# w2's gradient computed transposed, in two sets of PSUM banks, and turned in the last stage; bulk loads spread; turned queries stored sooner

## The chip, the cores and the metric

The kernel runs on one core of a Trainium2 chip. The metric is the device time of the whole program in microseconds (us); before the change three runs gave 822.75 to 823.58 us, median 823.29. A core has a matrix engine (TensorE, PE in the profile; its weight loads are PEld), three engines for other arithmetic (VectorE = DVE, ScalarE = ACT, GpSimd = POOL) and SyncE (SP), which here only issues transfers. Each engine works through its own list of instructions in order. PE writes to PSUM, eight banks of 512 floats on each of 128 partitions; ACT or DVE must copy a finished sum out before its bank can be used again. Transfers between DRAM and the on-chip memory SBUF are issued by SP, ACT or POOL and run beside the engines; some of them transpose what they move.

## The reference, cut to what matters

One transformer block (linear attention with 32 heads, then a gated MLP) is computed forward, and then its gradients for the input and five weight matrices. Sequence 2048, model width D = 640, MLP width F = 1728, all bf16.

```python
x = A_x
h = x + _A_ref(_layernorm(x, axis=-1), A_wqkv, A_wo)
h2 = h + _B_ref(_layernorm(h, axis=-1), B_w1, B_w3, B_w2)

def _B_ref(x, w1, w3, w2):
    gate = jnp.einsum("bsd,df->bsf", x, w1)
    up = jnp.einsum("bsd,df->bsf", x, w3)
    h = _silu(gate) * up
    out = jnp.einsum("bsf,fd->bsd", h, w2)
    return out
```

The change concerns above all the gradient of w2, an array of 1728 x 640: `h` transposed (1728 x 2048) times the gradient of the output (2048 x 640), a sum over the 2048 positions.

## The kernel before

The order of the work is written out by hand (`tc.manual_schedule()`): what stands later in the code comes later in the list of its engine. Tiles come from pools; a tile that takes over the place of another waits until all users of the old one are done. Positions are cut into 16 tiles of 128 (`t`), D into 5 chunks of 128 (`DT`), F into 13 chunks of 128 and one of 64.

The stages, with their times in the profiled execution:

1. **Projections** (0 to about 73 us, L458 to L638). For each position tile: statistics on DVE (`stat`, L480), normalising (`p1_norm`, L246; tiles 10, 12 and 14 on ACT, the others on DVE), turning (tiles 0 to 7 on PE, tiles 8 to 15 by a transposing transfer, L250), the projection on PE (`p1_mm`, L273), exp and relu on ACT (`phi`, L289). The list of DVE's steps beside tile t is `v_steps` (L508): S is `stat`, N `p1_norm`, R a remaining piece of `phi`; A, B and L place a normalising step before the query tile, after it, or last. SP's loads of x (L194, L461, L464), wqkv, w1, w3 (`w13`, L499), w2 and wo stand in front of this loop, in its dictionary `trickle` (L505) and after it (L591 to L594). `kvT_block` (L443) needs the last third of wqkv (`load_wq(4, 6)`) and the turned sums `mT`.
2. **Attention, second part** (73 to 98 us, the list given to `run`, L945). `q_late` projects the last query tiles into `pkx`; `q_out` (L724) stores tiles 10 to 13 from there through POOL's queue; `f2_wT` makes the matrix `Wp`, which `f2_half` multiplies with the turned queries. Then the pool `p1`, which holds `pkx`, is released, and the pool `pa` of the MLP takes its place.
3. **MLP forward and the gradients inside it** (98 to 340 us, L1003).
4. **Gradient of w2** (340.54 to 399.44 us, L1041 to L1111). `load_hh` turns four column blocks of the stored `h` into tiles `hb` (position on the partitions). For each of 13 chunks of 128 columns of F two sums of 16 matmuls are made: a block of `hb` as weights, 320 columns of the output gradient `g2` as the moving side. ACT copies each [128 x 640] result and stores it to the output `out_6`. The last 64 columns are done in `gw2_tail`, two halves side by side in the array. SP loads the next stage's weights (`load_w13`) and gradients (`load_gg`) meanwhile.
5. **Backward through the MLP and the attention** (399.44 to 699.5 us, L1257 to L1545). `b_ghn` (L1134) begins it, with PSUM tiles in the banks of stage 4. Its first steps need `ggb[0]` and the turned w1 and w3; `b_ln` then needs the loads of `b_load` (L1129).
6. **Gradients of w1 and w3** (699.5 to 816 us, L1548 to L1562). Seven blocks of up to 496 columns; for each block five jobs of 16 matmuls (`grad_job`), copied out by ACT and stored through ACT's queue. After each block SP loads the block after the next, by a transposing transfer, into the tile that has just come free.

Every transfer of SP and ACT counts up, when it lands, one of eight counters, which the program uses in turn; a transfer may not start before the one that used its counter last has landed. POOL's transfers have eight of their own.

Of the kernel before, what the change touches and what calls it, by code (L numbers as in the profile page):

```python
# [9 lines left out]
P = 128  # L10
BF16 = mybir.dt.bfloat16
F32 = mybir.dt.float32
# [6 lines left out]
S, D, H, F = 2048, 640, 32, 1728  # L19
DH = D // H  # L20
ST, DT = S // P, D // P
FT, FP = 14, 1792
FL = F - 13 * P
W, SC, TPC = 512, 4, 4
HD = D // 2
NG = 27
# [29 lines left out]
def kernel(  # L56
# [19 lines left out]
    V, A, T, G, SY = nc.vector, nc.scalar, nc.tensor, nc.gpsimd, nc.sync  # L76
# [20 lines left out]
    kvT_d = dram.tile([D, D], BF16, name="kvT_d")  # L97
    dwoT_d = dram.tile([D, D], BF16, name="dwoT_d")
    hn_d = dram.tile([S, D], BF16, name="hn_d")
    hh_d = dram.tile([F, S], BF16, name="hh_d")  # L100
# [81 lines left out]
    def load_wq(a, b):  # L182
        dma(out=wqkv[:, :, a * HD:b * HD], in_=wq_v[:, :, a * HD:b * HD])

    def load_x(a, b):
        dma(out=x_sb[:, a:b, :], in_=xS[:, a:b, :])
# [6 lines left out]
    load_x(3, 4)  # L193
    load_x(4, 8)  # L194

# [31 lines left out]
    def load_w13(c0, c1):  # L227
        def go1():
            dma(out=w1[:, c0:c1, 0:F], in_=rows(B_w1)[:, c0:c1, :])

        def go3():
            dma(out=w3[:, c0:c1, :], in_=rows(B_w3)[:, c0:c1, 0:F - FL])
        return [go1, go3]
# [198 lines left out]
    def m_end(m, js=(0, 1)):  # L432
        mb = mbs[:, m % 4, :]
        acc = macc[m]
        for j in js:
            A.copy(out=mb[:, j * HD:(j + 1) * HD], in_=acc[j][:, 0:HD])
        if m < 2:
            A.copy(out=Z[:, m:m + 1], in_=acc[1][:, HD:HD + 1])
            z_diag(m)
        if m < DT - 1:  # L440
            dmaT(out=mT[:, :, m * P:(m + 1) * P], in_=mb)
# [18 lines left out]
    load_g2T(0)  # L460
    load_x(8, 12)  # L461
    load_w2T(2 * P, 4 * P)
    load_wq(0, 2)
    load_x(12, ST)  # L464
    def warm_up(n, warm):
# [36 lines left out]
    def load_wo():  # L502
        dma(out=wo[:], in_=A_wo.rearrange("(c p) n -> p c n", p=P))

    trickle = {4: w13[0], 5: w13[1], 9: lambda: load_wq(4, 6), 12: w13[2], 14: w13[3]}  # L505

    R = None
    v_steps = {1: (R, ("N", 4)), 2: (("S", 5), R, ("N", 5)), 3: (("S", 6), R, ("N", 6), ("C", 0)),  # L508
               4: (("S", 7), R, ("N", 7), ("S", 8)), 5: (R, ("N", 8), ("S", 9)), 6: (R, ("N", 9), ("S", 10)),
               7: (("S", 11), R, R, ("A", 10), ("L", 11)), 8: (("S", 12), R, R, ("S", 13)),  # L510
               9: (("N", 13), R, ("S", 14), ("B", 12)), 10: (R, R, ("S", 15)), 11: (R, ("B", 14), ("L", 15))}
    V_OPS = {"S": stat, "N": p1_norm, "C": p1_scale}
# [8 lines left out]

    outs = {7: ((xn_out, 0, dma),), 8: ((group_out, 0),), 12: ((group_out, 1), (xn_out, 1, dma)), 13: ((group_out, 2),)}

# [66 lines left out]
    m_end(1)  # L590
    load_wo()  # L591
    group_out(SC - 1)
    for go in w13[4:]:
        go()  # L594
    z_late((2, 3, 4), big())
# [5 lines left out]
    m_part(2, range(10, ST))  # L601
    m_end(2)
    dmaG(out=m_v[:, 0, :], in_=mbs[:, 0, :])
    r_head(0)
# [336 lines left out]
    def kv3():  # L941
# [5 lines left out]
        (f2_wT, 4), (phi_rest,), (q_late, 14), (r_T, 4), (r_head, 5), (r_prod, 7),  # L947
        (mlp_ghh, 4),
        (q_late, 15), (w2_room,), (sig_table,), (f2_half, 0, 0), (f2_half, 1, 0), (f2_half, 2, 0), (f2_half, 3, 0), (mlp_ghh, 5),
        (f2_half, 0, 1), (r_store, 4, 5), (f2_half, 1, 1), (f2_hn, 0), (r_store, 5, 6), (f2_half, 2, 1), (f2_hn, 1),  # L950
        (f2_half, 3, 1), (f2_m_out,), (q_out, 10, 14),
        (f2_half, 4, 0, True), (mlp_ghh, 6), (f2_half, 4, 1, True), (f2_half, 5, 0, True), (r_red, 6, (0,)), (f2_hn, 2), (f2_hn, 3),
# [28 lines left out]
    def r_end(t):  # L981
        r_scale(t)
        r_out(t)

    r_steps = [{0: ((load_x, 6, 8),), 1: ((r4_out, 0, 2),), 2: ((r_load, 8),), 3: ((load_w2T, 10 * P, F),), 4: ((r_load, 9), (r4_out, 2, 4)),
                5: ((r_store, 7, 8),),
# [53 lines left out]

    hb, blk = {}, [(0, 512), (512, 512), (1024, 512), (1536, 192)]  # L1041

    def load_hh(b):
        f0, fw = blk[b]
        hb[b] = U2.tile([P, ST, 512], BF16, name="hb", tag="ABCA"[b])
        for a, n in ((0, 2 * P), (2 * P, 2 * P)) if b == 0 else ((0, fw),):
            dmaT(out=hb[b][:, :, a:a + n], in_=hh_d[f0 + a:f0 + a + n, :])

# [23 lines left out]
    def load_gg(j, c0, c1, q=dma):  # L1072
        if c0 == 0:
            ggb[j] = ba.tile([P, NG, 2 * P], BF16, name="ggb", bufs=2)
        q(out=ggb[j][:, c0:c1, :],
            in_=gg_d[c0 * P:c1 * P, j * 2 * P:(j + 1) * 2 * P].rearrange("(c p) w -> p c w", p=P))

    def gw2_tail():

        gt = ps.tile([P, 2, 512], F32, name="gt", tag="gw", bufs=4)  # L1080
        for t in range(ST):
            for j in range(2):
                T.matmul(gt[j * FL:(j + 1) * FL, 0, 0:HD], lhsT=hb[3][:, t, P:P + FL],
                         rhs=g2[:, t, j * HD:(j + 1) * HD], start=(t == 0), stop=(t == ST - 1))
        ob = br.tile([P, HD], BF16, name="gts")
        A.copy(out=ob[:], in_=gt[:, 0, 0:HD])
        for j in range(2):
            A.dma_start(out=out_6[F - FL:F, j * HD:(j + 1) * HD], in_=ob[j * FL:(j + 1) * FL, :])

    for fc in range(FT - 1):  # L1090
        b, i = divmod(fc, 4)
        if fc == FT - 2:
            gw2_tail()
        acc = ps.tile([P, 2, 512], F32, name="gw", bufs=4)
        for j in range(2):
            for t in range(ST):
                T.matmul(acc[:, j, 0:HD], lhsT=hb[b][:, t, i * P:(i + 1) * P], rhs=g2[:, t, j * HD:(j + 1) * HD],  # L1097
                         start=(t == 0), stop=(t == ST - 1))
        ob = br.tile([P, D], BF16, name="gw2o", bufs=2)
        A.copy(out=ob[:].rearrange("p (j n) -> p j n", j=2), in_=acc[:, :, 0:HD])  # L1100
        A.dma_start(out=out_6[fc * P:(fc + 1) * P, :], in_=ob[:])
        if fc == 3:
            load_hh(3)
        if fc == 5:
            load_w13()
        if fc == 8:
            load_gg(0, 0, NG)
        if fc == 11:
            load_gg(1, 0, NG)
    ps.release()  # L1110
# [440 lines left out]
    dmaT(out=g_h[:, 0:DT, :], in_=dwoT_d[:, :])  # L1551
    dma(out=out3S, in_=g_h[:, 0:DT, :])
    for i, (f0, f1) in enumerate(blocks):
        n = f1 - f0
        for m in range(DT):
            last = (i, m) == (len(blocks) - 1, DT - 1)
            for a, b in ((0, n - P), (n - P, n)) if last else ((0, n),):
                c = (a + b) // 2
                halves = ((a, c), (c, b)) if i * DT + m < 5 else ((a, b),)
                out = [(x + y - a, z + y - a, to) for y, w in halves for x, z, to in both_grads(m, f0 + y, f0 + w)]  # L1560
                grad_job(hnN, m, lambda t: gb[i][:, t, a:b], b - a, out, A.dma_start)
        load_block(i + 2)  # L1562
    ps.release()
    ex.release()
# [34 lines left out]
```

## Time and profile before

| what | value |
|---|---|
| median of 3 runs | 823.29 us |
| the profiled execution, time | 820.91 us |
| its span, first to last instruction | 819.1 us |
| granted clock of PE | 1.000 |
| PE busy | 814.1 us, 5420 matmuls |
| DVE, ACT, POOL busy | 452.4, 323.6, 130.9 us |
| gradient of w2, 416 matmuls of 320 columns | 56.8 us busy |
| its tail, 32 matmuls | 2.29 us of the chain |
| last stage, 576 matmuls | 116.65 us of the chain |

Times are from the start of the span. The profile has, among others, busy times by engine, a chain of work that is followed back from the last instruction, groups of instructions, timelines of each engine, and for every transfer the time from its issue to its landing. A busy PE is one that has a matmul under way; whether it runs at its pace is seen from the time between the starts of matmuls.

### The profile page before, as it was taken

Reading aid. Unit: us, or ns where it says so; the run is one execution under the profiler, and the core shown is the slowest. Engines: PE = TensorE matmul, PEld = TensorE weight load, DVE = VectorE, ACT = ScalarE, POOL = GpSimd, SP = SyncE. Lnnn points to the kernel's source line nnn. Section 1 sums busy time; section 2 is a strip of 40 time slices with the busy share of each in tenths; the row PEclk is TensorE's granted clock in tenths of the full one; section 3 lists DMA queues with packets and bytes.
Section 4 is the critical chain, followed back from the end, with each engine's and each line's share of the span. In section 5 each row is a group of like instructions: output and inputs, shape, how many; then the busy total and the mean of one; then the engine's idle time right before and its main releaser. Section 6 shows DMA issues by size and latency. Waiting matters only on the chain.

```text
span 819.1 us, 13944 instructions
## 1 busy us (share of the span) xinstructions
PE 814.1 (99%) x5420; PEld 512.8 (63%) x5420; DVE 452.4 (55%) x973; ACT 323.6 (40%) x603; POOL 130.9 (16%) x193
## 2 busy tenths in 40 slices
PE   9999999999999999999999999999999999999998
PEld 6677544555555555777777777777777777544444
DVE  7859987998898566300057777772781544200000
ACT  7856688665565666011122212222212334211111
POOL 2233333333222212100001111110220000000000
PEclk9999999999999999999999999999999999999999
DMA  9899699796485556999977877259974997967751
GB/s 264 219 290 239 166 244 327 225 245 173 127 211 156 169 170 167 222 261 226 257 176 180 211 197 200 58 107 187 287 195 93 181 194 159 239 164 186 160 141 36
DMA packets 323873, 157.88 MB, mean 193 GB/s; under 512 B 242784, under 2 KB 317056, under 8 KB 323808
## 3 DMA queue, kind: packets, MB, share of 16 engines
q1 hardware_dynamic: 281040, 116.18, 61.6%
q0 software_dynamic: 7328, 24.48, 8.7%
q10 hardware_dynamic: 35440, 16.34, 7.7%
q8 instruction: 42, 0.69, 0.4%
q14 instruction: 23, 0.19, 0.1%
HBM read 47.09 MB, written 51.13 MB: 120 GB/s over the span
## 4 chain that ended last, share of the span: by engine, by line
PE 96%; DVE 2%; ACT 1%; issue 0%; DMA 0%; POOL 0%; ACTq 0%; DVEq 0%
PE mm L394 20%; PE job L1346 20%; PE ghn L1142 14%; PE gxn L1515 8%; PE gw L1097 7%; PE o L910 4%; PE o L856 3%; PE gwo L1230 3%; PE big L267 3%; PE gr L1199 3%; PE dkv L1452 3%; PE macc L429 2%; PE at L654 2%; PE mm L267 1%; PE dkv L1380 1%; DVE st L147 1%
## 5 line engine op out<-in xcount | busy, mean ns | idle before, releaser
L1346 PE MATMUL job<-gb,hnN 128*128 128x496 bf16 (+3 forms) x576 | 116.8, 366 | 0.0
L1142 PEld LDWEIGHTS <-ggb 128*128 128x128 bf16 x864 | 84.5, 98 | 32.8
L1346 PEld LDWEIGHTS <-hnN 128*128 128x128 bf16 x576 | 55.8, 98 | 61.0
L394 PE MATMUL mm<-pqT,w 128*128 128x512 bf16 x405 | 93.8, 379 | 0.1
L394 PEld LDWEIGHTS <-w 128*128 128x128 bf16 x540 | 52.5, 98 | 63.4 <-issue 1.4
L1350 ACT CAST obs<-job 128x496 bf16<-128x496 f32 (+4 forms) x56 | 28.5, 510 | 123.7 <-PE job L1346 120.9
L1142 PE MATMUL ghn<-w13a,ggb 128*128 128x320 bf16 x448 | 63.5, 299 | 0.0
L1157 DVE SCALAR_TENSOR_TENSOR wb<-gs,hnb 128x640 f32<-128x640 bf16 x16 | 13.2, 825 | 88.7 <-ACT gs L1154 88.7
L1142 PE MATMUL ghn<-w13b,ggb 128*128 128x320 bf16 x416 | 61.4, 299 | 0.0
L394 PE MATMUL mm<-g2T,w2T 128*128 128x512 bf16 x240 | 59.6, 379 | 0.0
L1097 PE MATMUL gw<-g,hb 128*128 128x320 bf16 x416 | 56.8, 299 | 0.0
L1207 POOL TENSOR_TENSOR sz<-Zb,g_h 128x640 f32<-128x640 bf16 x16 | 20.2, 1261 | 197.7 <-DVE g_h L1208 197.7
L1097 PEld LDWEIGHTS <-hb 128*128 128x128 bf16 x416 | 40.6, 98 | 16.0 <-issue 0.3
L419 ACT CAST ghh<-mm 128x512 bf16<-128x512 f32 x48 | 28.3, 589 | 47.7 <-PE mm L394 40.1
L793 ACT ACTIVATE sig<-mm 128x512 bf16<-128x512 f32 x56 | 33.9, 605 | 26.4 <-PE mm L394 21.1
L1154 ACT ACTIVATE gs<-ghn 128x640 bf16<-128x640 f32 x16 | 11.3, 704 | 78.8 <-PE ghn L1142 73.9
L394 PEld LDWEIGHTS <-w2T 128*128 128x128 bf16 x260 | 25.4, 98 | 23.4
L267 PEld LDWEIGHTS <-pqT 128*128 128x128 bf16 x320 | 30.7, 98 | 13.7 <-ACT pqT L259 1.5
L267 PE MATMUL big<-wqkv,pqT 128*128 128x320 bf16 x250 | 38.6, 299 | 0.6 <-ACT pqT L259 0.3
L1346 PEld LDWEIGHTS <-g 128*128 128x128 bf16 x320 | 31.0, 98 | 11.5
L829 DVE TENSOR_TENSOR gate<-gate,sig 128x1024 bf16<-128x1024 bf16 x28 | 19.3, 689 | 33.2 <-ACT gate L804 30.5
L910 PE MATMUL o<-w,hhT 128*128 128x320 bf16 x224 | 35.0, 299 | 0.0
(219 smaller groups left out, 1369.9 us busy)
## 6 DMA issues: line engine op xcount, KB each, us to landing
hh_d<-hhT SPq DMA_DIRECT2D x24, 256.0 KB, 2.7
gg_d<-gate POOLq DMA_DIRECT2D x24, 256.0 KB, 4.3
gg_d<-ghh POOLq DMA_DIRECT2D x24, 256.0 KB, 3.4
ggb<-gg_d SPq DMA_DIRECT2D x6, 896.0 KB, 5.4
ggb<-gg_d ACTq DMA_DIRECT2D x6, 832.0 KB, 5.7
ggb<-gg_d SPq DMA_DIRECT2D x2, 1728.0 KB, 12.7
x_sb<-in_A_x_dram SPq DMA_DIRECT2D x5, 640.0 KB, 5.9
pk_d<-pk_all SPq DMA_DIRECT2D x4, 640.0 KB, 6.6
```

What stands on the lines that cost most here:

```text
L267: T.matmul(acc, lhsT=pqT[:, c, t * P:(t + 1) * P], rhs=wqkv[:, c, n0:n0 + HD], start=(c == 0), stop=(c == DT - 1))
L394: T.matmul(acc[:], lhsT=w[:, c, fc * P:(fc + 1) * P], rhs=rhs[:, c, :], start=(c == 0), stop=(c == DT - 1))
L419: A.copy(out=ghh[n // 2][:, n % 2, :], in_=acc[:])
L793: A.activation(sig[:, i, :], gp[:], AF.Sigmoid)
L856: T.matmul(accs[i, j][:, 0:HD], lhsT=hhT[c][:, fc, i * P:(i + 1) * P], rhs=w2[:, fc, j * HD:(j + 1) * HD], start=(first and fc == 0), stop ...
L910: T.matmul(o2["ps"][:, 0:HD], lhsT=hhT[c][:, fc, i * P:(i + 1) * P], rhs=w2[:, fc, j * HD:(j + 1) * HD], start=(fc == 0), stop=(fc == FT - 1))
L1097: T.matmul(acc[:, j, 0:HD], lhsT=hb[b][:, t, i * P:(i + 1) * P], rhs=g2[:, t, j * HD:(j + 1) * HD], start=(t == 0), stop=(t == ST - 1))
L1142: T.matmul(acc[:, j, 0:HD], lhsT=ggb[t // 2][:, k, lo:lo + P], rhs=rhs[:, j * HD:(j + 1) * HD], start=(k == 0), stop=(k == NG - 1))
L1199: T.matmul(gr[t][:, j, 0:HD], lhsT=ghT[t][:, c, :], rhs=wT2[:, c, j * HD:(j + 1) * HD], start=(c == 0), stop=(c == DT - 1))
L1346: T.matmul(acc[:, 0:n], lhsT=lhs[:, t, m * P:(m + 1) * P], rhs=rhs(t), start=(t == 0), stop=(t == ST - 1))
L1350: A.copy(out=ob, in_=acc[:, 0:n])
L1515: T.matmul(acc[:, j, 0:HD], lhsT=g, rhs=wqT[:, k, j * HD:(j + 1) * HD], start=(k == 0), stop=(k == 14))
```

## The change

- **Gradient of w2 turned round.** The four column blocks become 256, 448, 512 and 512 wide. For each block and each of the 5 chunks of D one sum of 16 matmuls is made, now with 128 columns of `g2` as weights and the whole block of `hb` as the moving side: 20 sums of up to 512 columns, with no tail of its own. The result is the gradient transposed; ACT copies and stores it to a scratch array `gw2T_d` in DRAM. The sums use two sets of four PSUM banks (`gw0`, `gw1`). POOL clears the padding of the block of 448.
- **Last stage.** After blocks 0 to 3 of the last stage SP loads a part of `gw2T_d` back by a transposing transfer into a free part of `g_h` (`gw2_turn`), and one block later stores it to `out_6` (`gw2_out`). Two more jobs store their result in halves.
- **Loads.** x comes as tiles 4-5, 6-9, 10-15 instead of 4-7, 8-11, 12-15. The second piece of w3 is cut in two. `load_wq(4, 6)` moves from tile 9 of the loop to the place of `load_wo`, `load_wo` and the last weight pieces move to after `m_end(2)`, one weight piece moves from tile 14 to after the loop. The first store of `pk` comes one tile later. Tile 14 is normalised by ACT before the query tile instead of after it. Two steps of the MLP's load list change places.
- **Query store.** `q_out(10, 14)` comes after `r_prod(7)` instead of at the end of the attention's list.

```diff
-    load_x(4, 8)
+    load_x(4, 6)
...
-        def go3():
+        def go3(c0=c0, c1=c1):
...
-    load_x(8, 12)
+    load_x(6, 10)
     load_w2T(2 * P, 4 * P)
     load_wq(0, 2)
-    load_x(12, ST)
+    load_x(10, ST)
...
-    trickle = {4: w13[0], 5: w13[1], 9: lambda: load_wq(4, 6), 12: w13[2], 14: w13[3]}
+    trickle = {4: w13[0], 5: lambda: w13[1](0, 1), 6: lambda: w13[1](1, 2), 12: w13[2]}
...
-               9: (("N", 13), R, ("S", 14), ("B", 12)), 10: (R, R, ("S", 15)), 11: (R, ("B", 14), ("L", 15))}
+               9: (("N", 13), R, ("S", 14), ("B", 12)), 10: (R, R, ("S", 15)), 11: (R, ("A", 14), ("L", 15))}
...
-    outs = {7: ((xn_out, 0, dma),), 8: ((group_out, 0),), 12: ((group_out, 1), (xn_out, 1, dma)), 13: ((group_out, 2),)}
+    outs = {7: ((xn_out, 0, dma),), 9: ((group_out, 0),), 12: ((group_out, 1), (xn_out, 1, dma)), 13: ((group_out, 2),)}
...
-    load_wo()
+    load_wq(4, 6)
     group_out(SC - 1)
-    for go in w13[4:]:
-        go()
+    w13[3]()
...
     m_end(2)
+    load_wo()
+    for go in w13[4:]:
+        go()
...
-        (mlp_ghh, 4),
+        (q_out, 10, 14), (mlp_ghh, 4),
...
-        (f2_half, 3, 1), (f2_m_out,), (q_out, 10, 14),
+        (f2_half, 3, 1), (f2_m_out,),
...
-    hb, blk = {}, [(0, 512), (512, 512), (1024, 512), (1536, 192)]
+    hb, blk = {}, [(0, 256), (256, 448), (704, 512), (1216, 512)]
...
+    for n in range(len(blk) * DT):
+        b, m = divmod(n, DT)
+        f0, fw = blk[b]
+        tag = "gw0" if n // 4 in (0, 2) or n in (16, 17) else "gw1"
+        acc = ps.tile([P, 512], F32, name="gw", tag=tag, bufs=4)
         for t in range(ST):
+            T.matmul(acc[:, 0:fw], lhsT=g2[:, t, m * P:(m + 1) * P], rhs=hb[b][:, t, 0:fw], start=(t == 0),
+                     stop=(t == ST - 1))
+        ob, fp = br.tile([P, 512], BF16, name="gw2o", bufs=3), (fw + P - 1) // P * P
+        if fp > fw:
+            G.memset(ob[:, fw:fp], 0.0)
+        A.copy(out=ob[:, 0:fw], in_=acc[:, 0:fw])
+        A.dma_start(out=gw2T_d[m * P:(m + 1) * P, b * 512:b * 512 + fp], in_=ob[:, 0:fp])
+        if n == 4:
             load_hh(3)
+        if n == 9:
             load_w13()
+        if n in (12, 15):
+            load_gg((n - 12) // 3, 0, NG)
...
+    turned = [DT, DT + 2, DT + 6, 0]
+
+    def gw2_turn(b):
+        n = (blk[b][1] + P - 1) // P
+        dmaT(out=g_h[:, turned[b]:turned[b] + n, :], in_=gw2T_d[:, b * 512:b * 512 + n * P])
+
+    def gw2_out(b):
+        f0, fw = blk[b]
+        n, k = fw // P, turned[b]
+        dma(out=out_6[f0:f0 + n * P, :].rearrange("(k p) d -> p k d", p=P), in_=g_h[:, k:k + n, :])
+        if fw % P:
+            dma(out=out_6[f0 + n * P:f0 + fw, :], in_=g_h[0:fw % P, k + n, :])
...
-                halves = ((a, c), (c, b)) if i * DT + m < 5 else ((a, b),)
+                halves = ((a, c), (c, b)) if i * DT + m < 7 else ((a, b),)
...
         load_block(i + 2)
+        if 0 < i <= 4:
+            gw2_out(i - 1)
+        if i < 4:
+            gw2_turn(i)
```

More of the change, by code (lines that the diff above doesn't have):

```diff
@@ L98 @@
     dwoT_d = dram.tile([D, D], BF16, name="dwoT_d")
+    gw2T_d = dram.tile([D, 4 * 512], BF16, name="gw2T_d")
     hn_d = dram.tile([S, D], BF16, name="hn_d")
@@ L983, in r_end @@
         r_out(t)
-    r_steps = [{0: ((load_x, 6, 8),), 1: ((r4_out, 0, 2),), 2: ((r_load, 8),), 3: ((load_w2T, 10 * P, F),), 4: ((r_load, 9), (r4_out, 2, 4)),
+    r_steps = [{0: ((load_x, 6, 8),), 1: ((r4_out, 0, 2),), 2: ((load_w2T, 10 * P, F),), 3: ((r_load, 8),), 4: ((r_load, 9), (r4_out, 2, 4)),
                 5: ((r_store, 7, 8),),
@@ L1045, in load_hh @@
         hb[b] = U2.tile([P, ST, 512], BF16, name="hb", tag="ABCA"[b])
-        for a, n in ((0, 2 * P), (2 * P, 2 * P)) if b == 0 else ((0, fw),):
-            dmaT(out=hb[b][:, :, a:a + n], in_=hh_d[f0 + a:f0 + a + n, :])
+        dmaT(out=hb[b][:, :, 0:fw], in_=hh_d[f0:f0 + fw, :])
     load_hh(0)
@@ L1076, in load_gg @@
             in_=gg_d[c0 * P:c1 * P, j * 2 * P:(j + 1) * 2 * P].rearrange("(c p) w -> p c w", p=P))
-    def gw2_tail():
-        gt = ps.tile([P, 2, 512], F32, name="gt", tag="gw", bufs=4)
-        for t in range(ST):
[L1082 to L1102, printed above, removed]
+    for n in range(len(blk) * DT):
[3 more added lines that the diff above has]
+        acc = ps.tile([P, 512], F32, name="gw", tag=tag, bufs=4)
+        for t in range(ST):
+            T.matmul(acc[:, 0:fw], lhsT=g2[:, t, m * P:(m + 1) * P], rhs=hb[b][:, t, 0:fw], start=(t == 0),
[6 more added lines that the diff above has]
+        if n == 4:
             load_hh(3)
-        if fc == 5:
+        if n == 9:
             load_w13()
[L1106 to L1109, printed above, removed]
+        if n in (12, 15):
+            load_gg((n - 12) // 3, 0, NG)
     ps.release()
```

## The prediction

> **What bounds the kernel now.** I read the page first, then the chain of waits in order of time, then the timelines and the waits of the engines that feed PE at each edited place.
>
> ```profile
> PE 814.1 (99%) x5420; PEld 512.8 (63%) x5420; DVE 452.4 (55%) x973; ACT 323.6 (40%) x603; POOL 130.9 (16%) x193
> ...
> PE 96%; DVE 2%; ACT 1%; issue 0%; DMA 0%; POOL 0%; ACTq 0%; DVEq 0%
> ```
>
> PE is the bound from end to end, and it runs at its pace. Between starts of successive matmuls of one line the trace has 136 ns at 320 columns, 209 at 496 and 216 at 512: 0.4167 ns a column plus 2.5 ns each. Summed by that rule over the 5420 matmuls this makes 814.6 us of the 819.1; some 1.1 us pass before the first matmul, about 3 us after the last, and the lost time between amounts to under 3 us, nearly all in the first 14 us, plus 0.28 us at 37.7 and 0.28 at 102. So a change can gain only what it takes from PE's own sum or from these few stalls, and loses whatever new stall it makes.
>
> ```profile
> 340.54 52.16 PE gw L1097 x384
> 392.70 2.29 PE gt L1083 x32
> 394.99 4.45 PE gw L1097 x32
> 399.44 19.56 PE ghn L1142 x144
> ```
>
> This is the chain (start, length, what). The w2 stage takes 399.44 - 340.54 = 58.90 us without a gap.
>
> **Part 1, the w2 sums.** Removed: 58.90 us. Added: 5 chunks x 16 = 80 matmuls for each block. By the pace above a matmul takes 109.2 ns at 256 columns, 189.2 at 448 and 215.8 at 512: 80 x 109.2 = 8.74, 80 x 189.2 = 15.14, 160 x 215.8 = 34.53, together 58.40 us. The columns streamed are the same (138,240); gained are 112 starts of 2.5 ns and the tail's 143 ns for each pair of half-width matmuls. **-0.50 us.** The weight load of 98 ns lies under every one of these matmuls (109 ns at least), as now under 136. ACT's 20 copies (a 512-wide copy is 0.59 us at L419) and 20 issues of 0.35 us make 19 us in 58: hidden.
>
> The Trainium skill ("TensorE: Matmul & The Clock Gate", section "Back-to-back issue gap") gives 131 ns as the sustained gap at 512 columns. By that figure the two wide blocks alone would shrink by 160 x 85 ns = 13.6 us. The trace has 216 ns in 748 such gaps, so the sum goes by 216.
>
> **Part 2, do the blocks arrive in time?** SP's list:
>
> ```profile
> 329.51 34.37 SPq L1047 DMA_TRANSPOSE hb<-hh_d  x5
> 363.94 9.75 SPq L1066 DMA_TRANSPOSE w13a<-in_B_w_dram  x1
> 373.91 12.30 SPq L1067 DMA_TRANSPOSE w13b<-in_B_w_dram  x1
> 386.27 1.27 SPq L1068 DMA_TRANSPOSE w13a<-w13tail  x1
> 387.84 4.77 SPq L1075 DMA_DIRECT2D ggb<-gg_d  x2
> 392.71 7.87 SPq L1131 DMA_DIRECT2D hnb<-hn_d  x1
> ```
>
> From issue to landing the first three pieces of hb take 10.0, 9.6 and 13.1 us, so 256 columns are there at 339.5, 512 at 344.8, 1024 at 353.8. Needed now: 349.2 for the second 256, 357.9 for the next 512, over 4 us to spare each. After: columns 256 to 704 are one transfer, needed at 340.54 + 8.74 = 349.28. Between the landings above, 704 columns are there at 344.8 + 9.0 x 192/512 = 348.2; if a partial square of 64 costs a full one, at 349.3. The spare time shrinks to 0 to 1.1 us, while stores begin 3 us sooner than now. Bounds 0 to +1; I take **+0.1**. The later blocks have 7 us and more.
>
> The Trainium skill ("DMA: Bandwidth & Descriptors", "Issuing engines are not separate DMA queues") says that transfers of all queues share the same 16 engines, so ACT's stores slow SP's transposes. By that the two 64 KB stores issued ahead of the landing cost this transfer 128 KB at the 234 to 266 GB/s of 340 to 350, 0.5 us: 348.7, still before 349.28.
>
> **Part 3, the hand-over to the next stage.** A transfer waits until the one eight before it, of SP and ACT together, has landed. This already holds ACT here:
>
> ```profile
> ACT gw2o L1100 <- DMA out_dram<-gw2o: 13.2, 3, 5.0
> ACT gw2o L1100 <- DMA w13b<-in_B_w_dram: 2.9, 1, 2.9
> ```
>
> The store at 388.58 starts 0.08 us after w13b's landing, the one at 405.13 after hnb's (392.7 + 12.3 = 405.0). A waiting store has the next copies behind it on ACT, and PE waits for these only when it needs the bank. After, 20 stores lie among the same loads. Counting eight on from ggb[0] (landing 387.8 + 9.2 = 397.0) by the order in which the issues would stand, I reach the store of sum 16; the copy of sum 17 is then done near 398, and the next stage, which begins on the banks of sums 16 and 17, wants them at 398.9. Eight on from ggb[1] (landing 388.4 + 16.2 = 404.6) lies beyond copy 17. Bounds 0 to +6.3 (rival B); taken **0**.
>
> **Part 4, the start.** The S step of tile 6 runs with DVE full before it:
>
> ```profile
> 15.74 0.88 DVE L147 BATCH_NORM_STATS2 st<-x_sb 128x6 f32<-128x320 bf16 x2
> ```
>
> Tile 6 now comes with tiles 6 to 9, a load like the one issued at 11.25 that landed 4.8 us later, at 16.05; with two tiles fewer in front of it up to 1.3 us earlier (320 KB at 250 GB/s). Late by 0 to 0.4 us, and DVE's chain reaches PE near 37; **+0.1**. The cut w3 piece, the moved store and ACT's earlier tile 14 free transposes that are in time now (tile 9 lands at 25.8 + 4.6 = 30.4, wanted at 30.74): nothing gained in this execution, a stall less where they are late.
>
> **Part 5, loads moved past 55 us.** `load_wq(4, 6)` (800 KB, some 2.7 us of a full DMA) now runs where wo ran, so what follows is later by up to 2.7 us, less what the turned sum mT gains by going ahead of the last pieces. mT's fourth block lands at 68.3 + 5.5 = 73.8, wanted at 75.64; Wp's third at 82.5 + 2.6 = 85.1, wanted at 85.45. wqkv's last third is wanted at 64.2 and should land near 60 to 62. Bounds 0 to +2.4; between 65 and 70 the trace's DMA moves only 146 GB/s, so part of the delay is absorbed: **+0.2**.
>
> **Part 6, the query store.**
>
> ```profile
> 96.15 2.67 DMA pq_d<-pkx
> 98.82 1.86 issue
> 100.68 0.04 ACTq L793
> ...
> 102.45 4.48 PE mm L394 x20
> ```
>
> The chain runs from this store to ACT's first sigmoid, which had stood idle 2.0 us, and PE loses 0.28 us at 102. After, POOL issues it behind the product ending at 85.96; it lands near 90, when DMA is 60% busy, and behind it on POOL nothing waits before 91.7. ACT's copy `up` still may wait for DVE's reduction of tile 7 (ending 101.6), so 0 to -0.28: **-0.2**.
>
> **Part 7, the last stage.**
>
> ```profile
> 717.00:734.00 17.00, 17.00 (x83) 7.93 (x82) 0.00 (x0) 2.86 (x5) 0.00 (x0) 1.00 0.66 157
> ```
>
> (Columns end with clock, DMA share and GB/s.) A block is 16.7 us of PE; its load is issued at the block's start and lands 10.9 us later. Each added turn stands behind that load on SP: at most 20 squares, where the 25 of `g_h<-dwoT_d` took 4.4 us to issue and 7.1 to land. 10.9 + 7.1 is past the block's end, but then only the next load is behind, with 5.8 us to spare. ACT's two more issues of 0.35 us lie in its idle time, eight banks deep. **0**, at worst +0.5.
>
> Sum: -0.50 + 0.1 + 0 + 0.1 + 0.2 - 0.2 + 0 = **-0.3 us**: the profiled execution's 820.91 becomes 820.6, and with the 2.38 us by which the median stands above it, **823.0 us**. Own range of this case 822.0 to 824.3.
>
> **Rivals.** *A, a late block or Wp* (parts 2 and 5): PE stands up to 1.0 us at 349.3 and up to 2.4 us at 75 to 85, of which the sum already holds 0.3: 823.0 + 3.1 = 826.1 at most, 824.6 at half. For it: spare times of 0.3 to 1.1 us. Against: no such stall now. *B, ACT held by a counter*: should copy 17 stand behind a store that waits for ggb[1], it ends at 404.6 + 0.6, 6.3 us after 398.9: 829.3. It decides from one place in the order of issues; my count misses it by two. *C, faster*: the three runs are 2.4 us above the profiled execution. If that is stalls at the transposes that are 0.25 to 0.3 us early in the trace, parts 4 and 6 remove them: down to 823.0 - 2.4 = 820.6, likelier 821.3. Against: the trace can't show it. *D, 131 ns at 512 columns* (the figure weighed in part 1): 809.
>
> **Chances.** Forecast 0.58, A 0.15 (a third of it under 0.2%), B 0.07, C 0.19, D 0.01. What counts as a difference is 0.2%, 1.65 us. Faster: C and D, 0.20. Slower: 0.10 of A, 0.07 of B, and 0.04 out of the forecast's 0.58 for a stall in the last stage that I have not seen: 0.21. Within: 0.54 and the rest of A, 0.59. For 8 in 10 the range takes in most of A and C: 820.7 to 826.0; B and D stay out.
>
> **What would show it.** The w2 stage at 58.4 us and the chain at 398.9 for the next stage (part 1); no gap of PE at 349 (2), none at 398.9 (3); PE starts at 37.7 and 75 to 86 as now (4, 5); sigmoid about 2 us earlier (6); seven equal blocks of 16.7 us at the end (7). A gap of over 1 us at any of these makes the prediction wrong.

## The result, and the profile after

| | before | changed |
|---|---|---|
| median of 8 runs each, on one chip, us | 823.08 | 820.25 |
| lowest and highest | 822.29, 826.29 | 819.32, 822.72 |
| ratio, 95% interval | | 0.9969 (0.9959 to 0.9979) |
| profiled execution: time, span | 820.91, 819.1 | 820.36, 818.6 |

By the ratio the changed kernel is 0.31% faster, some 2.6 us, where the forecast was 0.3 us; its time lies 0.45 us below the low end of the range. The two profiled executions differ by only 0.5 us. Before's stands below all of its eight timed runs, the changed kernel's in the middle of its own. This decides how everything else is read.

The page after (busy times by engine, then the chain of waits in shares):

```profile
PE 811.6 (99%) x5261; PEld 501.6 (61%) x5292; DVE 452.7 (55%) x973; ACT 324.8 (40%) x609; POOL 131.7 (16%) x198
...
PE 96%; DMA 1%; ACT 1%; DVE 1%; issue 0%; SPq 0%; POOL 0%; DVEq 0%
```

PE is still the bound. The work is now 5292 matmuls (5420 less 448 of the old w2 sums, plus 320), as the count of weight loads says too, and 31 of them have no record: each missing one shows as a hole of one 512-column start, 216 ns, and is no stall. The chain after, as start, length, what:

```profile
340.21 24.08 PE gw L1086 x161
...
398.61 19.56 PE ghn L1131 x144
...
699.31 116.65 PE job L1335 x576
```

The w2 stage takes 398.61 - 340.21 = 58.40 us, to the hundredth as summed; the last stage has its 116.65 us as before. ACT's waits between 340 and 400 (engine, tile and line, what it waited for: us in total, times, longest):

```profile
ACT gw2o L1091 <- DMA w13b<-in_B_w_dram: 7.3, 1, 7.3
...
ACT gw2o L1091 <- DMA ggb<-gg_d: 3.5, 1, 3.5
```

ACT's stores do stand behind the counters, and the longest wait of a copy behind such a store is 7.3 us. The store of sum 16 starts at 395.63, after the first `ggb` has landed at 395.56; those of sums 17 and 18 follow at 396.68 and 397.74, and the next one to be held, by `hnb`, is that of sum 19. PE waits for none of it. PE's own new waits are two (timeline: start, length, engine, line, operation, operands, count, and in brackets the idle time and what ended it):

```profile
85.57 2.60 PE L657 MATMUL at<-Wp,pqT 128*128 128x320 bf16 x18 [0.24 <-DVE rden L378]
```

```profile
566.50 0.78 PE L1388 MATMUL gkvT<-tri,woT 128*128 128x140 bf16 x10 [0.47 <-DMA tri<-tri]
```

Against the pace these are 0.40 and 0.63 us. The releaser named in the first is not the one: the reciprocal ended at 85.35, while Wp's third block landed at 85.48, 0.09 us ahead of the product. The two stalls of before, 0.28 us each at 37.7 and 102, are gone. So this pair of traces explains 0.5 us; 2 us more must be in executions of before that the first trace does not show.

### The profile page after: what moved, and what is told of

Read it like the earlier page. It is cut to its first block, busy times and chain, and to the rows that moved or that the text cites. A ratio compares the mean times of both kernels' runs of the same rounds, so it can differ in the third digit from the quotient of the medians.

```text
span 818.6 us, 13711 instructions
## 1 busy us (share of the span) xinstructions
PE 811.6 (99%) x5261; PEld 501.6 (61%) x5292; DVE 452.7 (55%) x973; ACT 324.8 (40%) x609; POOL 131.7 (16%) x198
## 4 chain that ended last, share of the span: by engine, by line
PE 96%; DMA 1%; ACT 1%; DVE 1%; issue 0%; SPq 0%; POOL 0%; DVEq 0%
PE mm L395 20%; PE job L1335 19%; PE ghn L1131 14%; PE gxn L1504 8%; PE gw L1086 7%; PE big L268 4%; PE o L913 4%; PE o L859 3%; PE gwo L1219 3%; PE macc L430 3%; PE gr L1188 3%; PE dkv L1441 3%; PE at L657 2%; DMA wqkv<-in_A_wqkv_dram 1%; PE dkv L1369 1%; DMA tri<-tri 1%
## 5 line engine op out<-in xcount | busy, mean ns | idle before, releaser
L1086 PE MATMUL gw<-hb,g 128*128 128x512 bf16 (+2 forms) x316 | 58.4, 345 | 0.2
L1086 PEld LDWEIGHTS <-g 128*128 128x128 bf16 x320 | 31.3, 98 | 27.0
L268 PEld LDWEIGHTS <-pqT 128*128 128x128 bf16 x320 | 30.7, 98 | 13.5 <-ACT pqT L260 0.9
L1335 PEld LDWEIGHTS <-g 128*128 128x128 bf16 x320 | 31.0, 98 | 11.5
L1091 ACT CAST gw2o<-gw 128x512 bf16<-128x512 f32 (+2 forms) x20 | 10.4, 519 | 66.6 <-PE gw L1086 25.3
```

Source lines behind the costliest of these rows:

```text
L268: T.matmul(acc, lhsT=pqT[:, c, t * P:(t + 1) * P], rhs=wqkv[:, c, n0:n0 + HD], start=(c == 0), stop=(c == DT - 1))
L1086: T.matmul(acc[:, 0:fw], lhsT=g2[:, t, m * P:(m + 1) * P], rhs=hb[b][:, t, 0:fw], start=(t == 0), stop=(t == ST - 1))
L1335: T.matmul(acc[:, 0:n], lhsT=lhs[:, t, m * P:(m + 1) * P], rhs=rhs(t), start=(t == 0), stop=(t == ST - 1))
```

## The experiments

Every kernel was timed against before on the same chip, and its profile read for PE's gaps over the pace of 0.4167 ns a column plus 2.5 ns. w3_double, gg_early and b_third have one time each. Some names in the expectations are wrong. What they call turned or transposed queries is a turned tile of the normalised input x (`pqT<-x_sb`), which the projection multiplies with wqkv; the one called tile 5 is tile 9, and in hybrid2 the one called tile 9 is tile 14. The times given with them are right.

**Whose gain is it?** Before once more, and the change in three pieces: the w2 sums with their turning (`gw_only`), the loads with the order around them (`loads_only`), the query store (`qout_only`). One telling edit of gw_only and one of loads_only, and the whole edit of qout_only, in this order:

```diff
-    hb, blk = {}, [(0, 512), (512, 512), (1024, 512), (1536, 192)]
+    hb, blk = {}, [(0, 256), (256, 448), (704, 512), (1216, 512)]
...
-    trickle = {4: w13[0], 5: w13[1], 9: lambda: load_wq(4, 6), 12: w13[2], 14: w13[3]}
+    trickle = {4: w13[0], 5: lambda: w13[1](0, 1), 6: lambda: w13[1](1, 2), 12: w13[2]}
...
-        (mlp_ghh, 4),
+        (q_out, 10, 14), (mlp_ghh, 4),
...
-        (f2_half, 3, 1), (f2_m_out,), (q_out, 10, 14),
+        (f2_half, 3, 1), (f2_m_out,),
```

> The kernel before, unchanged: another profiled execution and more times. The profiled execution that the prediction was made from took 820.9 us where the eight timed ones took 822.3 to 826.3. Theory S (the typical execution of the kernel before holds stalls of PE of some 2 us that this profiled one lacks): a span of 820.5 to 822 us with some 1.5 to 2.5 us more between the starts of matmuls, in the first 105 us. Theory N (no such stalls; the times differ outside the span): a span of 819.1 again. Ratio 1.000.

> Only the transposed w2 sums, their scratch array and the turning in the last stage; loads and query store as before. Theory S: -0.5 us, ratio 0.9994 (0.9988 to 1.0002). Rival W (the gain comes from the w2 stage and its hand-over, where a typical execution of before waits): -2 us or more, ratio 0.9976 or less.

> Only the moved and cut loads, the earlier normalising of tile 14 and the later store of pk; w2 stage and query store as before. Theory S: most of the gain, -1.5 to -2.2 us, ratio 0.9973 to 0.9982. Rival W: -0.2 to +0.3 us, ratio 0.9998 to 1.0004.

> Only the query store moved ahead. Theory S: 0 to -0.3 us, ratio 0.9996 to 1.0000. Rival Q (the store delays the MLP's first tiles by more in a typical execution than the 0.28 us of the profiled one): -1 us or more, ratio 0.9988 or less.

Measured, with 822.50 as the median of before on that chip:

| kernel | median, us | ratio, 95% interval | span of its trace |
|---|---|---|---|
| b_again | 822.01 | 0.9996 (0.9984 to 1.0009) | 822.0 |
| gw_only | 821.01 | 0.9983 (0.9970 to 0.9997) | 818.8 |
| loads_only | 822.39 | 1.0001 (0.9988 to 1.0014) | 820.5 |
| qout_only | 821.38 | 0.9990 (0.9976 to 1.0003) | 819.6 |

Theory N falls: time less span is 1.7 to 1.8 us in every profiled execution of this study, so the runs differ inside the span. Rival W wanted 2 us or more from the w2 stage; gw_only has 1.5 by the median, but in its trace the w2 stage is 0.51 us shorter and no more, with 0.24 at the program's end, so W falls. Rival Q wanted 1 us or more from the query store; qout_only has 1.1 by the median and 0.8 by the ratio, whose interval includes no gain at all, so the times alone do not settle it. S was wrong that the loads alone bring the gain: the trace of loads_only is as short as the changed kernel's up to 51 us, but it stands 0.60 us at 85 and 0.96 at 102, and its program's end takes 0.41 us longer. S was right that the stalls exist, and the second trace of before, 2.9 us longer than the first, shows them (1.26 us of it stands at 131 to 136, which is taken up at the end of this section). SP's list there and PE's timeline:

```profile
24.57 0.58 SPq L232 DMA_DIRECT2D w<-in_B_w_dram  x1
25.74 6.44 SPq L250 DMA_TRANSPOSE pqT<-x_sb  x3
```

```profile
32.05 1.67 PE L267 MATMUL big<-wqkv,pqT 128*128 128x320 bf16 x11 [1.22 <-DMA pqT<-x_sb]
...
104.16 0.59 PE L394 MATMUL mm<-pqT,w 128*128 128x512 bf16 x2 [0.76 <-ACT up L800]
```

At 24.57 SP issues w3's uncut piece (832 KB). The transfer that turns tile 9 is issued next, at 25.74. The piece lands at 29.97 and tile 9 at 32.00; PE wanted it near 30.7. In the first trace of before it landed at 30.46, and PE went on; its 0.28 us at 37.7 are another wait, for ACT's copy of a tile that was turned on PE:

```profile
30.74 2.88 PE L267 MATMUL big<-wqkv,pqT 128*128 128x320 bf16 x20
...
PE big L267 <- ACT pqT L259: 0.3, 1, 0.3
```

In the changed kernel, with half the piece ahead of it, tile 9 lands at 29.06 and PE goes on too:

```profile
24.64 0.58 SPq L233 DMA_DIRECT2D w<-in_B_w_dram  x1
25.80 1.20 SPq L251 DMA_TRANSPOSE pqT<-x_sb  x1
27.05 0.58 SPq L233 DMA_DIRECT2D w<-in_B_w_dram  x1
```

```profile
30.74 2.88 PE L268 MATMUL big<-wqkv,pqT 128*128 128x320 bf16 x20
```

The Trainium skill ("DMA: Bandwidth & Descriptors", section "Two DMAs through the same engine are not ordered") says that within one queue of one DMA engine descriptors start in order, and that a later one may complete before an earlier one has finished writing. The trace agrees with the start in order: in b_again the first packet of tile 9 starts at 28.82, 3.1 us after its issue, while the piece's packets start from 25.80 to 29.47; in the changed kernel it starts at 27.60. How long after the piece the tile lands is not a matter of the piece's size alone: 0.7 us behind every half piece, 0.7 and 0.8 us behind the two whole pieces that landed first (29.40 and 29.65), and 2.0 to 2.1 us behind the five that landed at 29.89 or later. What makes this step of 1.3 us is not shown.

The second stall is the query store. ACT in b_again and, below it, in the changed kernel:

```profile
102.54 0.60 ACT L793 ACTIVATE sig<-mm 128x512 bf16<-128x512 f32 x1 [2.68 <-PE mm L394]
```

```profile
99.13 0.60 ACT L796 ACTIVATE sig<-mm 128x512 bf16<-128x512 f32 x1 [0.21 <-ACT x_sb L662]
99.62 0.59 ACT L797 ACTIVATE s<-mm 128x512 bf16<-128x512 f32 x1
101.40 0.59 ACT L803 CAST up<-mm 128x512 bf16<-128x512 f32 x1 [1.19 <-DVE rden L374]
```

The profile names a matmul as releaser, but in all eight traces that have the store in its old place the first sigmoid starts 0.22 or 0.23 us after the store has landed (b_again 102.32 and 102.54, before 100.61 and 100.84, w3_double 106.06 and 106.28). The landing comes 3.7 to 4.4 us after the issue's end, and PE's gap behind it is 0.28 to 1.18 us. With the store moved both are gone, in all nine traces. So what rival Q says of the cause holds in the traces.

**Is it the piece of w3?** The cut alone; all moved loads without it; the changed kernel with the cut as its only moved load; the changed kernel again. The line for split_only, which gw_qout_split has too, and the one for loads_nosplit:

```diff
+    trickle = {4: w13[0], 5: lambda: w13[1](0, 1), 6: lambda: w13[1](1, 2), 9: lambda: load_wq(4, 6), 12: w13[2], 14: w13[3]}
...
+    trickle = {4: w13[0], 5: w13[1], 12: w13[2]}
```

> Before, with one part of the change: w3's piece for chunks 0 and 1 is loaded as two halves in steps 5 and 6, and all else stays. Theory S2 (a stall that comes and goes): in before PE loses 1.4 us at 30.5 in some executions, 0.3 at 37.6 in others, since the transposed queries of tile 5 queue behind the uncut piece (they landed at 32.0 and 31.9 us in two traces, at 30.5 and 30.1 in two others); with the cut they land near 29.1 as in the changed kernel, so no gap over 0.15 us at 30.5 or 37.6, and the median falls by 0.5 to 1.0 us, to 821.5 to 822. The gap at 102 (0.3 to 1.0 us) stays. Rival U (the stall hangs on how fast the first loads come, not on the cut): the gap at 30.5 or 37.6 stays in this trace, and the time is that of before. Rival V (what is saved at 30.5 is lost again by 105): the gaps go, others of the same sum come at 85 or 102, and the time is that of before.

> Before with all moved loads of the change but w3's cut, whose piece stays whole in step 5. Theory S2: the stall at 30.5 (up to 1.4 us) or 37.6 (0.3) is back, and the one at 85 for Wp's transpose (0.4 to 0.6 us in both traces with the moved loads) stays, so this is slower than before by 0.3 to 0.8 us: 822.8 to 823.3. Rival U: no stall at 30.5, since tiles come in another order; time as with all the loads moved, 822.4.

> The changed kernel with only w3's cut kept of the moved loads. Theory S2: it has the gains (w2 sums 0.5, program end 0.28, the stall at 102 of 0.3 to 1.0, the one at 30.5 of 0.3 to 1.4) without the gap of 0.4 us at 85 for Wp: 0.4 us below the changed kernel, about 819.9, no gap over 0.15 us at 30.5, 85 or 102. Rival W2 (the moved loads gain in other places too): not below the changed kernel, 820.3 to 821, with gaps between 50 and 100 that the changed kernel does not have.

> The changed kernel once more, unchanged. Theory S2: 820.0 to 820.6 by the median, about 2.3 us below before on the same chip, with no gap at 30.5, 37.6 or 102, with the gap at 85 (0.3 to 0.6 us); the gap at 565.8 (0.63 us in its first trace, a turned block behind a store of POOL) shows whether it belongs to the kernel or to that execution. Rival N (times differ outside the span): span and time differ by another amount than the 1.75 us of the earlier runs.

Measured, before's median 822.23: split_only 822.55 us, 1.0004 (0.9995 to 1.0013); loads_nosplit 822.43, 0.9999 (0.9989 to 1.0009); gw_qout_split 820.07, 0.9973 (0.9962 to 0.9983); after_again 819.70, 0.9973 (0.9962 to 0.9983).

The stall at 30.5 follows the cut, as S2 has it, and rival U falls: loads_nosplit has tile 9 at 32.54 and a gap of 2.03 us, split_only has it at 29.36 and no gap at 30.5. But the times do not follow: split_only is not 0.5 to 1.0 us faster than before, and loads_nosplit is not slower than it (its trace is of the second slowest of its eleven runs). So no timed pair shows what the cut is worth by itself. PE's waits from 20 to 110 us in split_only:

```profile
PE bigx L448 <- DMA mT<-hx: 0.3, 1, 0.3
PE mm L394 <- ACT up L800: 0.3, 1, 0.3
```

It keeps the 0.28 us at 37.7, which S2 had put down to the piece: this gap is in all five traces that load x as before and have no stall at 30.5, with the cut or without, and in none of those with x in the new order. And mT's third block lands at 69.01, which costs 0.45 us at 68.5 (before's landed at 68.08, in time); also its program takes 3.65 us from the last matmul to the end, 0.43 more than before. That is rival V in part: the cut takes one stall away and what is behind wo becomes the next. The moved wo is what clears 68.5 (the block lands at 66.5 in the changed kernel), and Wp's third block pays for it at 85. In after_again the gap at 85 is back with 0.44 us, the one at 566 is not. That one belongs to single executions: hybrid (below) has it again with 0.40 us, the seven other traces with the new w2 sums and the eight with the old ones have not. gw_qout_split was to be 0.4 us below the changed kernel; it is 0.37 above, within the intervals. It has no gap at 85, but 0.29 us at 37.6 and 0.57 at 68.4, which rival W2 had as its sign.

**A dose, a third look at before, the counters, and a better mix.** The edits of w3_double (to before), gg_early and hybrid (both to the changed kernel):

```diff
+    trickle = {5: lambda: (w13[0](), w13[1]()), 9: lambda: load_wq(4, 6), 12: w13[2], 14: w13[3]}
...
-        if n in (12, 15):
-            load_gg((n - 12) // 3, 0, NG)
+        if n in (11, 12):
+            load_gg(n - 11, 0, NG)
...
+    trickle = {4: w13[0], 5: lambda: w13[1](0, 1), 6: lambda: w13[1](1, 2), 9: lambda: load_wq(4, 6), 12: w13[2], 14: w13[3]}
...
-    load_wq(4, 6)
     group_out(SC - 1)
-    w13[3]()
```

> Before, with w1's first piece (885 KB) moved from step 4 to step 5, so that it and w3's uncut piece (852 KB) are both issued at 24.6 ahead of the turned queries of tile 5. Theory S2 (the queries queue behind what is issued ahead of them): they land not at 30.1 to 32.0 but at 33 to 36, PE stands 2.3 to 5 us at 30.5, and the span is 821.5 to 825. Rival U (the stall hangs on the first loads, not on this piece): the gap at 30.5 stays under 1.5 us.

> Before, unchanged, one more profiled execution. Theory S2: one of two forms at the start, tile 5's queries landing near 31.9 with a gap of 1.2 to 1.4 us at 30.5, or near 30.3 with one of 0.3 at 37.6; at 102 a gap of 0.3 to 1.0 us that ends 0.2 us after the query store has landed; program end 0.35 us between POOL's last two semaphore instructions. A span of 819.1 as in the first profile is at the low end, 820 to 822 is likelier.

> The changed kernel with both ggb loads issued after sums 11 and 12 in place of 12 and 15, so that the second is nearer to the first in the order of issues. Theory of part 3 and rival B: a store of ACT waits for the landing of the transfer eight before it. In the changed kernel the store of sum 16 waits for the first ggb (starts 395.63, landing 395.56) and that of sum 19 for hnb (402.53 after 402.45), and PE loses nothing. If the second ggb (landing near 401.7) now stands eight ahead of a store of sums 13 to 16, the copy of sum 17 comes behind it, and PE stands 2 to 6 us ahead of the stage that begins near 398.4. Rival Y: ACT's waits are long but the banks are free soon enough, no gap above 0.2 us between 395 and 405.

> The changed kernel, with the last third of wqkv and w3's second piece loaded early again, in steps 9 and 14 as before, while wo and the last pieces stay behind the third M part, where the change has put them. Theory S2: the gap at 85 (0.40 and 0.44 us in two traces of the changed kernel) is the backlog of these two loads, so Wp's third block lands before 85.3 and the gap is under 0.1; the gap at 68.4 (0.45 to 0.57 us in three traces where wo is loaded ahead of mT) stays away, mT's third block landing near 66; no new gap. Its median is 0.2 to 0.4 us below the changed kernel's, about 819.4 to 819.8. Rival X (Wp's blocks wait for their own producers, not for the loads): the gap at 85 stays at 0.4 and the time is that of the changed kernel.

w3_double: span 824.6, tile 9 at 34.20, inside S2's bounds. PE at 30.5, the gap being 3.60 us against the pace:

```profile
34.24 1.50 PE L267 MATMUL big<-wqkv,pqT 128*128 128x320 bf16 x9 [3.44 <-DMA pqT<-x_sb]
```

b_third: span 821.5, tile 9 at 32.46. PE's waits in its first 140 us, those of S2:

```profile
PE big L267 <- DMA pqT<-x_sb: 1.3, 1, 1.3
...
PE mm L394 <- ACT up L800: 1.0, 1, 1.0
```

Landings of tile 9 and PE's gap at 30.5, over all traces but gg_early, whose first tiles ran 1.6 us late:

| w3's piece | landing, us | gap, us |
|---|---|---|
| whole | 30.08 (gw_only), 30.46 (first trace) | none; 0.31 and 0.28 at 37.6 |
| whole | 31.89, 32.00, 32.46, 32.54 | 1.26, 1.38, 1.44, 2.03 |
| whole, behind w1's piece | 34.20 | 3.60 |
| cut | 28.93 to 29.56 (nine traces) | none; 0.28 to 0.30 at 37.6 in the three with x as before |

gg_early (820.87 us, one run) settles nothing about rival B: the turned tail of w1 stands ahead of both loads in SP's list, so they were issued no earlier than elsewhere, the first one 46.5 us after the start of the w2 sums (43.8 to 47.3 in the other traces of the new sums), and the order of the stores stayed. It shows only that ACT may wait 9.2 us at a stretch there without a gap of PE between 390 and 408.

hybrid: 821.82 us, 0.9980 (0.9968 to 0.9991), before being 823.23. No gap at 68 or 85, but a new one of 1.90 us at 44.5, of the same kind. SP's list and PE:

```profile
38.86 0.57 SPq L521 DMA_DIRECT2D pk_d<-pk_all  x1
39.49 0.50 SPq L184 DMA_DIRECT2D wqkv<-in_A_wqkv_dram  x1
40.96 2.72 SPq L251 DMA_TRANSPOSE pqT<-x_sb  x2
```

```profile
46.56 0.72 PE L268 MATMUL big<-wqkv,pqT 128*128 128x320 bf16 x4 [1.74 <-DMA pqT<-x_sb]
```

**One store's place, and the candidates side by side.** hybrid2 is hybrid with the first store of `pk` back where before has it, ahead of tiles 12 and 13 (issued at 33.5 in place of 38.9); the other two repeat kernels.

```diff
-    outs = {7: ((xn_out, 0, dma),), 9: ((group_out, 0),), 12: ((group_out, 1), (xn_out, 1, dma)), 13: ((group_out, 2),)}
+    outs = {7: ((xn_out, 0, dma),), 8: ((group_out, 0),), 12: ((group_out, 1), (xn_out, 1, dma)), 13: ((group_out, 2),)}
```

> As hybrid, with the first group store of pk back in step 8, where before has it. In hybrid the queries of tile 9 landed at 46.5 us behind this store and the last third of wqkv, both issued at 38.9 to 40.0, and PE stood 1.9 us at 44.5; in before, with the store issued after these queries, they landed at 44.4 without a gap. Theory S2 (turned queries queue behind what SP issues ahead of them): the gap at 44.5 goes, those at 30.5, 68.4, 85 and 102 stay away, and the median is 0.2 to 0.5 us below the changed kernel's on this chip. Rival X2 (wqkv's third alone is enough): the queries still land after 45.5 and a gap of 0.5 us or more stays at 44.5.

> The changed kernel with only w3's cut kept of the moved loads, once more, beside the changed kernel on the same chip. Theory S2: gaps of 0.3 at 37.6 and 0.5 at 68.4 in place of the changed kernel's 0.4 at 85, so within 0.5 us of it, either way. Rival Z (the other moved loads gain more than the traces show): the changed kernel is 0.6 us or more below.

> The changed kernel unchanged, for the two runs beside it: 2.2 to 2.6 us below before, a gap of 0.3 to 0.5 us at 85, none at 30.5, 68.4 or 102.

Before's median 823.04: hybrid2 819.84 us, 0.9960 (0.9948 to 0.9973); gwqs_again 821.15, 0.9970 (0.9958 to 0.9983); after_third 819.54, 0.9960 (0.9945 to 0.9976). With the store no longer beside it, the last third of wqkv lets tile 14 through:

```profile
38.69 0.57 SPq L184 DMA_DIRECT2D wqkv<-in_A_wqkv_dram  x1
41.15 2.52 SPq L251 DMA_TRANSPOSE pqT<-x_sb  x2
```

It lands at 44.81 in place of 46.52, and PE takes it at 44.85. X2 falls on the gap, but there are only 0.04 us to spare. hybrid2 has none of the listed gaps and is still not the 0.2 to 0.5 us faster than the changed kernel that S2 wanted. The product with Wp begins at 85.70 us in it, at 85.57, 85.62 and 85.27 in the changed kernel: Wp's third block lands at 85.50, as there, and the gap is gone only because PE comes later. To this extent rival X stands. after_third has only 0.21 us at 85, less than forecast. gwqs_again has its gaps at 37.6 and 68.4 and, besides, 1.03 us at 131 to 134 and 0.58 at 148.6, which the other trace of the same kernel has not. By its median it is 1.6 us behind after_third, past the 0.6 us that rival Z named; the two intervals overlap, and on the earlier chip the difference was 0.37 us. No version here beats the changed kernel.

The gap at 131 speaks for Z. It is in two of the seventeen traces, b_again and gwqs_again, and both have the MLP's load list in the order of before. In b_again, the transfer that ACT waited for (from the chain of waits), ACT's copy and PE:

```profile
123.37 10.50 DMA gg_d<-ghh
...
133.95 0.58 ACT L419 CAST ghh<-mm 128x512 bf16<-128x512 f32 x1 [2.86 <-PE mm L408]
...
134.59 1.24 PE L394 MATMUL mm<-pqT,w 128*128 128x512 bf16 x5 [0.70 <-ACT ghh L419]
136.05 0.81 PE L394 MATMUL mm<-pqT,w 128*128 128x512 bf16 x3 [0.23 <-ACT up L800]
```

ACT's copy takes the place of an earlier tile, which POOL stores to `gg_d`. It starts 0.08 us after the landing of that store in all ten traces in which it has to wait, so the matmul that is named is not the releaser. The store runs beside SP's transposing load of `g2T`. Counted from the MLP's first turn at 96, this load is issued at 24.4 to 25.6 us in the nine traces with the old order and at 22.2 to 23.5 in the eight with the two steps exchanged (the last of the change's edits of the loads). The store takes 5.8 to 10.5 us in the nine and ACT waits for it in eight of them, 0.5 to 2.9 us; in the eight it takes 6.4 to 7.8 us, and ACT waits in two, at most 0.16 us. PE stands only where the store took over 10 us. The exchange was never made alone, and other traces of the same two kernels have no such gap; that the exchange removes it is likely and not shown, and Z stays open.

## Why the prediction was wrong

These are three profiled executions of before and three of the changed kernel. Each row runs from the end of the row above to the first matmul of what it names, so that the row to 399 holds the w2 stage. The lengths in us, in the order in which they were taken:

| stretch, to about | before | changed | mean change |
|---|---|---|---|
| first sums, 51 | 51.77, 52.82, 53.28 | 51.50, 51.51, 51.39 | -1.16 |
| product with Wp, 85 | 33.67, 33.67, 33.83 | 34.07, 34.11, 33.88 | +0.30 |
| MLP's first turn, 96 | 10.35, 10.35, 10.35 | 10.32, 10.33, 10.33 | -0.03 |
| first gradient product, 143 | 47.11, 48.92, 47.81 | 46.68, 46.68, 46.68 | -1.26 |
| w2 stage, 340 | 197.47, 197.47, 197.47 | 197.46, 197.47, 197.47 | 0 |
| backward, 399 | 58.91, 58.91, 58.91 | 58.40, 58.40, 58.40 | -0.51 |
| 565 | 166.46, 166.47, 166.47 | 166.47, 166.47, 166.47 | 0 |
| 625 | 59.69, 59.70, 59.69 | 60.34, 59.69, 59.69 | +0.21 |
| last matmul, 815 | 190.48, 190.48, 190.48 | 190.48, 190.48, 190.48 | 0 |
| end | 3.22, 3.20, 3.22 | 2.91, 2.91, 2.92 | -0.30 |

Together -2.74 us (from unrounded lengths), which is what the medians have (2.5 to 3.5 us by chip). From 143 us to the last matmul before repeats itself to 0.01 us in all stages; all its spread is in the first 143.

**The step that failed** is the last of the sum: "the profiled execution's 820.91 becomes 820.6, and with the 2.38 us by which the median stands above it, 823.0 us". The 2.38 us were carried over as if the change could not touch them. They were for the most part stalls at the two places that parts 4 and 6 edit, absent or small in that one execution: against it b_again stands 1.10 us longer at 30.5 to 38 and 0.64 at 102, of 2.85 us in all, and b_third 1.17 and 0.90, of 2.38. The rest of b_again is mostly the gap at 131 to 136, at the exchanged steps of the MLP's load list, to which no part gave a term. Rival C said so and got 0.19, against it that "the trace can't show it". The forecast had the argument in hand that decides: every one of the three timed runs stood above the profiled one by at least 1.84 us, and in a trace that is 99% PE at its pace such a surplus is most likely waiting, which this trace has at the start and hardly elsewhere.

Point by point:

- **Part 1** (-0.50): measured -0.51. At the 131 ns that the Trainium skill ("TensorE: Matmul & The Clock Gate", section "Back-to-back issue gap") gives for 512 columns, the stage would have come to an estimated 44.8 us; it took 58.40, so rival D falls.
- **Part 2** (+0.1): 0. The block wanted at 349.28 landed at 347.08 in the first trace of the changed kernel, ahead of the estimate of 348.2 to 349.3.
- **Part 3** (0): 0, and the count was right: the store of sum 16 is held by the first `ggb`, the next held is beyond sum 17. That a nearer load would cost 6.3 us was not shown; the one attempt did not move it.
- **Part 4** (+0.1): the loss that it feared near 37 did not come; the gap at 37.7 is gone with x in the new order. The mechanism of the gain was named ("a stall less where they are late") and given nothing, because tile 9 landed 0.3 us early in the one trace. In four of six traces with the whole piece as before had it, PE stands 1.26 to 2.03 us for it. The stretch to 51 is 1.16 us shorter by the means of three traces each; no timed pair shows it.
- **Part 5** (+0.2): +0.30 by the means, at the place named: Wp's third block, summed as landing at 85.1, comes at 85.18 to 85.53. mT's fourth block costs nothing; the third one, which no part named, is late in some traces with wo ahead of it.
- **Part 6** (-0.2): the sigmoid starts 1.7 us earlier than in the first trace of before and 3.4 earlier than in the second, as forecast. The term was mis-sized: the gap that goes is 0.28, 0.92 and 1.18 us in the three traces, 0.79 in the mean. The stretch to 143, 1.26 us shorter, holds 0.42 more from the gap of 1.26 at 131 to 136 in b_again alone; that is not the query store's, since gwqs_again has it too with the store moved.
- **Part 7** (0): the jobs cost nothing. The +0.21 at 625 is the one gap of 0.63 at 566. No part had the -0.30 at the program's end.
- **Rivals**: A happened in small (the 0.2 to 0.44 us at 85); B and D did not; C did. At its full price, 820.6, it still lies 0.35 us above the measured 820.25, about what the program's end gave, which no part had.

Open: why the first loads differ from one execution to the next, what makes tile 9 land 0.7 or 2.0 us behind the piece, whether the exchanged steps of the load list remove the gap at 131, what makes the one at 566, and the program's end. Three traces of a kernel are also few for means.

## What to carry to other kernels

When the profiled execution is faster than every timed run, as here, its trace is close to the kernel's best case: suspect in the difference waits that it does not show, look for the transfers that arrive with less than half a microsecond to spare, and ask which of them the change touches. A transposing transfer that PE waits for should not be issued behind a bulk load on the same queue; cutting the load or moving a store by one step took 1 to 2 us of PE's waiting away here. What is freed at one such place is partly lost at the next (68, then 85 us), and the cut alone gained no time, so read the whole stretch, not the gap alone.

## What the runs showed of the hardware that was not expected

- A kernel whose work from 143 us to the last matmul repeats itself to 0.01 us spreads over 2.9 us between 0 and 143: 142.91, 145.76 and 145.28 us in three traces of before.
- The time from the start of the last matmul to the end of the span is a property of the program. It is 3.20 to 3.23 us in six traces with the old w2 sums, 3.63 and 3.65 in two others of these (loads_only and split_only, the two that cut w3's piece), 2.91 to 2.98 in all nine with the new sums, though the last matmuls and stores are the same. Part of it lies between the last two semaphore instructions of POOL: from 818.66 to 819.03 in before, from 818.46 to 818.54 in the changed kernel. The cause was not tried.
- The releaser that the profile names was wrong at both decisive waits of ACT and PE: a matmul for the store's landing at 102 (0.22 us before the sigmoid in eight traces), a reciprocal for Wp's block at 85 (0.09 us before the product in the three traces of the changed kernel). The constant distance to a landing gives the right one.
